# Clustered attention, a 2-D Fourier transform and a feed-forward network on one core: the transform in its own space beside the preceding sequence's last half block, and the normalization on other engines

## The chip, the cores and the metric

The kernel runs on one core of a Trainium2 chip. That core has five engines that work side by side: PE (matrix products; the trace shows its weight loads apart, as PEld), DVE (vector work), ACT (functions of one operand, scaled), POOL (GpSimd) and SP, which here only issues DMAs. Each engine takes its instructions in the order in which the program holds them. The metric is the device time of one execution in microseconds, lower being better. Of the kernel before there are three timed runs: 1066.58, 1066.92 and 1068.79 us, with a median of 1066.92 us.

## The reference, cut to what matters

```python
# q, k, v: (4, 8, 768, 64); centroids: (8, 16, 64); w_ch1: (512, 2048); w_ch2: (2048, 512)
q_assign = argmax(q_n @ c_n.T); k_assign = argmax(k_n @ c_n.T)     # unit vectors, per head
scores = where(q_assign[:, None] == k_assign, (q @ k.T) / 8, -1e9)
attn = softmax(scores) @ v                                          # (4, 768, 512) after joining heads
u = attn + real(fft(fft(attn, axis=seq), axis=model))
un = (u - mean(u)) / sqrt(var(u) + 1e-6)
out = u + relu(un @ w_ch1) @ w_ch2
```

Everything is held to about float32 accuracy: each product is made of float16 halves, a high and a low part, and three matmuls (high by high, high by low, low by high).

## The kernel before, in words

**Attention.** The 32 heads (4 sequences of 8) are taken in 16 pairs, and each pair in 6 blocks of 128 queries. So there are 96 steps, 24 for each sequence. A step's `scores` makes two tiles of 128x768 scores on PE, in two PSUM tiles of the pool `ps_big`, of which there are only two; DVE takes each row's maximum (L322, two instructions of a step, called the maxima here), ACT makes the exponentials (L328) and their high halves (L333), POOL the low halves (L334), a transposing DMA turns them round, and two steps later `attend` multiplies them by v. The two score tiles come free when ACT has made the exponentials; until then the next step's scores, first in PE's queue, wait, and with them all that PE has behind them.

**What follows a sequence's attention** is called its layer here. `fold` adds and subtracts mirrored rows and columns of the sequence X; its halves are transposed by DMA. `transform` then multiplies by cosine and sine tables: three accumulations of the odd part (L659 by way of `three`), three and one short one of the even part, each split into halves by ACT and DVE, and then three blocks t = 0, 1, 2 of a cosine and a sine pass. Their sums and differences dm and dp (L716, L717) are added to X (L723, L724); block 0 also makes one middle column. `norm` takes mean and variance of two row blocks and writes normalized rows as halves, which a DMA transposes (L756 to L769); `inverse` makes the factor that undoes its power-of-two scale (L776 to L783). `up` makes 16 feature blocks of 12 matmuls each (L798), of which ACT takes the rectified value in float32 (L802) and in float16 (L803) and POOL the rest (L804). `down` makes two outputs of 48 matmuls each (L818), yielded in pieces of 12; a piece costs 2.6 us in the planner's count. Norm, up and down come three times for a sequence, for two row blocks each, called half blocks here.

**Order.** PE's order is written out by the program: `Overlap.run` makes a table of steps, and after each step's scores and attend `fill` takes pieces of the layer of the sequence before, in proportion to what is left (`COST` 130 us over 24 steps). The other engines' orders are made by a scheduler from priorities; `high_priority` puts instructions ahead. At the end of a sequence `fold` is called, two steps later `drain` issues all that is left of the layer before, then the second part of `fold` (small transposes on PE), and `begin` starts the new layer. So on PE a layer is over before the next one's transform starts. The last sequence's layer has no attention beside it; it follows the rest of the third one's.

**Space.** One SBUF region, `arena`, serves the tables, the transform's parts and the feed-forward's activations by hand-set offsets. The tables `cs` and `ss` (577.5 KB each) lie at offset 0, where `up` keeps its activations, so they are loaded when the layer before has finished there.

The prediction's steps touch `Fourier.fold`, `tables`, `transform`, `FeedForward.norm`, `inverse`, `up`, `down` and `Overlap.layer`, `fill`, `drain`, `begin`, `run`.

## Time and profile before

| | |
|---|---|
| timed runs | 1066.58, 1066.92, 1068.79 us |
| the profiled execution | 1062.06 us, of which the span from first to last instruction is 1060.3 us |
| busy, of the span | PE 918.0 us (87%), ACT 635.9 (60%), DVE 601.3 (57%), POOL 569.3 (54%) |
| granted TensorE clock, mean | 0.934 of full speed |

The trace is of one execution, and its clock starts with the first instruction. Busy time of PE counts matmuls from issue to end, overlapping ones once, so 100% says that PE never waited, not that it ran at its peak. The granted clock has two levels here: 1.00 is 2.4 GHz and 0.50 is 1.2 GHz, and a mean between them tells the share of the time at each. The program's shape in time: attention with nothing of a layer beside it up to about 240 us; then three times a layer beside the next sequence's attention, with a change of layers near 240 to 300, 460 to 540 and 680 to 760 us; and from 884 us the last layers alone.

### The profile page before, as it was taken

What the parts mean: (1) busy time and instruction counts of PE and PEld (TensorE: products, weight loads), DVE (VectorE), ACT (ScalarE), POOL (GpSimd) and SP (SyncE); (2) the same over time, 40 slices, a digit from 0 to 9 for tenths busy, and PEclk for the clock granted to TensorE, in tenths of its full rate; (3) what the DMA queues carried; (4) which work ended last, traced back from release to release, by engine and by line L of the source; (5) the groups of instructions that cost most, each with busy time, mean ns of one, the idle gap of its engine ahead of it and who ended that gap; (6) DMA issues with size and microseconds to landing.
All of it is one profiled execution on the core that took longest, in us unless ns stands there. A gap on an engine that the chain in (4) does not pass through costs nothing.

```text
span 1060.3 us, 23530 instructions
## 1 busy us (share of the span) xinstructions
PE 918.0 (87%) x9349; PEld 598.4 (56%) x9362; DVE 601.3 (57%) x1325; ACT 635.9 (60%) x1051; POOL 569.3 (54%) x605
## 2 busy tenths in 40 slices
PE   3666565658799999998899999989899999699998
PEld 1243333335575766755666758556658575475674
DVE  8779897686955454568845454689354222710000
ACT  4798997855575766755766748556757472251340
POOL 1364565755684756655955657538737463341330
PEclk9987887868899999998999999998999999889999
DMA  7799998986778666788697656788666563211000
GB/s 267 180 218 235 204 251 186 177 163 126 152 116 183 120 135 124 135 154 155 123 174 132 136 120 131 132 160 158 110 132 108 98 112 62 67 30 36 11 11 21
DMA packets 381582, 141.58 MB, mean 134 GB/s; under 512 B 366104, under 2 KB 366112, under 8 KB 381472
## 3 DMA queue, kind: packets, MB, share of 16 engines
q1 hardware_dynamic: 381472, 140.08, 65.0%
q8 instruction: 73, 1.20, 0.5%
q14 instruction: 37, 0.30, 0.1%
HBM read 42.53 MB, written 6.29 MB: 46 GB/s over the span
## 4 chain that ended last, share of the span: by engine, by line
PE 55%; DVE 14%; DMA 12%; ACT 8%; issue 6%; POOL 5%; SPq 0%; POOLq 0%; ACTq 0%; DVEq 0%
PE ps_f L818 20%; PE ps_f L798 19%; PE ps_big L303 5%; DMA pt<-p 3%; DMA arena<-in_moe_w_ch_dram 3%; DMA pt<-ph 3%; POOL ph L334 2%; PE ps_o L354 2%; PE ps_o L356 2%; PE ps_o L355 2%; PE ps_f L659 2%; ACT p L328 2%; ACT ph L333 2%; DVE ju L322 1%; PE ps_big L308 1%
## 5 line engine op out<-in xcount | busy, mean ns | idle before, releaser
L334 POOL TENSOR_TENSOR ph<-p,ph 128x768 f16<-128x768 f32 x144 | 241.6, 1679 | 149.9 <-ACT ph L333 120.3
L798 PE MATMUL ps_f<-arena,w1h 128*128 128x256 f16 x1536 | 267.5, 275 | 17.6 <-DVE rt L782 10.7
L818 PE MATMUL ps_f<-w2h,arena 128*128 128x512 f16 x768 | 238.3, 379 | 0.0
L328 ACT ACTIVATE p<-ps_big,rmx,sce 128x768 f32<-128x768 f32 x144 | 142.5, 992 | 126.7 <-DVE ju L322 118.0
L322 DVE TENSOR_SCALAR_CACHE_REDUCE ju<-ps_big,sce 128x768 bf16<-128x768 f32 x144 | 145.9, 1013 | 116.2 <-PE ps_big L308 109.3
L798 PE MATMUL ps_f<-arena,w1l 128*128 128x256 f16 x768 | 211.1, 275 | 0.0
L804 POOL TENSOR_TENSOR arena<-arena 128x256 f16<-128x256 f32 x192 | 130.9, 687 | 135.3 <-ACT arena L803 132.9
L818 PEld LDWEIGHTS <-arena 128*128 128x128 f16 x1152 | 109.0, 98 | 126.4 <-issue 4.2
L354 PE MATMUL ps_o<-v,pt 128*128 128x66 f16 x1152 | 128.6, 201 | 49.3 <-DVE X L370 25.2
L798 PEld LDWEIGHTS <-w1h 128*128 128x128 f16 x1536 | 151.4, 99 | 35.0 <-issue 16.9
L303 PE MATMUL ps_big<-hlk,hlq 64*128 64x384 f16 x1152 | 132.6, 355 | 39.9 <-ACT p L328 26.9
L802 ACT ACTIVATE arena<-ps_f,wrel 128x256 f32<-128x256 f32 x192 | 92.2, 480 | 98.9 <-PE ps_f L798 73.9
L354 PEld LDWEIGHTS <-pt 128*128 128x128 f16 x1152 | 112.2, 101 | 64.0 <-issue 33.9
L818 PE MATMUL ps_f<-w2l,arena 128*128 128x512 f16 x384 | 145.5, 379 | 0.0
L355 PE MATMUL ps_o<-v,pt 128*128 128x64 f16 x1152 | 128.5, 201 | 0.0
L356 PE MATMUL ps_o<-v,pt 128*128 128x66 f16 x1152 | 128.1, 200 | 0.0
L333 ACT CAST ph<-p 128x768 f16<-128x768 f32 x144 | 119.9, 836 | 9.0 <-DMA pt<-ph 7.4
L303 PEld LDWEIGHTS <-hlq 64*128 64x128 f16 x1152 | 56.6, 100 | 102.7 <-issue 74.3
L355 PEld LDWEIGHTS <-pt 128*128 128x128 f16 x1152 | 112.7, 102 | 3.0
L356 PEld LDWEIGHTS <-pt 128*128 128x128 f16 x1152 | 113.1, 104 | 0.0
L803 ACT ACTIVATE arena<-ps_f,wrel 128x256 f16<-128x256 f32 x192 | 92.0, 479 | 0.0
L824 DVE SCALAR_TENSOR_TENSOR arena<-ps_f,rest,X 128x512 f32<-128x512 f32 x24 | 17.9, 746 | 129.7 <-PE ps_f L818 129.7
(169 smaller groups left out, 1332.7 us busy)
## 6 DMA issues: line engine op xcount, KB each, us to landing
arena<-in_moe_w_ch_dram SPq DMA_DIRECT2D x32, 512.0 KB, 5.9
scr<-in_q_dram SPq DMA_DIRECT2D x16, 384.0 KB, 3.2
scr<-in_k_dram SPq DMA_DIRECT2D x16, 384.0 KB
vst<-in_v_dram SPq DMA_DIRECT2D x16, 384.0 KB, 3.3
out_dram<-arena SPq DMA_DIRECT2D x24, 256.0 KB, 2.6
pt<-ph SPq DMA_TRANSPOSE x168, 3.9
arena<-in_cs_dram SPq DMA_DIRECT2D x4, 577.5 KB
arena<-in_ss_dram SPq DMA_DIRECT2D x4, 577.5 KB
```

The lines of the kernel that those rows point to most:

```text
L303: nc.tensor.matmul(out=ps[j][:, hf, 0:SH], lhsT=hq[rows[j], a, sl], rhs=hk[rows[j], c, hs], start=(i == 0), stop=False)
L322: nc.vector.tensor_scalar(out=ju, in0=ps[j][:, :, 0:SH], scalar1=ne, scalar2=None, op0=ALU.mult, op1=ALU.min, accum_out=m)
L328: nc.scalar.activation(x, ps[j][:, :, 0:SH], AF.Exp, bias=m, scale=e)
L333: nc.scalar.copy(out=ph[:, 0], in_=p32)
L334: nc.gpsimd.tensor_tensor(out=ph[:, 1], in0=p32, in1=ph[:, 0], op=ALU.subtract)
L354: nc.tensor.matmul(out=o[:, at:at + W], lhsT=hi, rhs=v16[:, kt, 0:W], start=(kt == 0), stop=False)
L355: nc.tensor.matmul(out=o[:, at:at + D], lhsT=hi, rhs=v16[:, kt, 66:130], start=False, stop=False)
L356: nc.tensor.matmul(out=o[:, at:at + W], lhsT=lo, rhs=v16[:, kt, 0:W], start=False, stop=(kt == ST - 1))
L798: nc.tensor.matmul(out=ps.rearrange("p (t x) -> p t x", x=P), lhsT=a[:, dc, fs], rhs=c[:, :, dc], start=(i == 0), stop=(i == 11))
L802: nc.scalar.activation(r, ps, AF.Relu, scale=rel[:, f:f + 1])
L804: nc.gpsimd.tensor_tensor(out=hl[:, f], in0=r, in1=hh[:, f], op=ALU.subtract)
L818: nc.tensor.matmul(out=ps, lhsT=a[:, f, ts], rhs=c[:, f], start=(i == 0), stop=(i == 47))
```

## The change

Three groups of edits. Line numbers of the changed kernel differ: `three` is L673, dm and dp L734 and L735, the additions to X L741 and L742, `norm` L774 to L788, `inverse` L795 to L802, the float32 rectification L822 or L824, `down`'s matmuls L847.

1. The transform gets offsets of its own: `arena` grows from 42176 to 47264 bytes, the tables `cs` and `ss` are loaded in thirds, each into space whose content has just been used, and `fold` does the odd part first. The layer before keeps its last pieces (`KEEP` 10.5, or `KEEP3` 7.9 before the last layer, counted in the planner's us), and `layer` hands them out between the transform's parts by the lists `MIX` and `MIX3`. The second part of `fold` comes one step after the first instead of two.
2. `norm`: the normalized rows are made by ACT instead of DVE; the low halves by POOL, but for the first of a sequence; the scale is computed for two rows at once. `inverse` is POOL's but for a reciprocal. Every second feature block of `up` is rectified in float32 by DVE instead of ACT. The additions to X of blocks 1 and 2 are all POOL's.
3. The layer's instructions are issued behind the latest maxima (`issue_after`), and norm 0 is called in block 1 of the transform, not after block 0; norm 2 in `down` of half block 0, not ahead of it.

```diff
-    CS, SS, CM, NY, XR, YN, MID = 0, 4640, 9280, 9824, 10592, 12160, 13216
-    XF, XT, XH, XM, XC, XL = 24640, (30816, 33888), 36960, 40128, 41184, 41216
-    FE = (0, 0, 1, 1)
-    UE = (1, 1, 0, 1)
+    CD, SD, XF, XT, XH = 20480, 22560, 24640, (30816, 33888), 36992
+    XM, XC, XL, XR, CM, YN, NY = 40160, 41216, 41248, 41280, 42848, 43392, 44448
+    CS, SS = (33888, 30816, 20480), (35456, 32352, 22016)
+    FOLDS = ((1, ALU.subtract), (0, ALU.add))
+    FE = (0, 0, 0, 1)
+    UE = (1, 1, 1, 1)
...
+    def third(self, t):
+        at = self.arena.at
+        n = P + (t == 0)
+        self.cs, self.ss = at(self.CS[t], [P, 2, 3, n], F16), at(self.SS[t], [P, 2, 3, P], F16)
+        for nm in ("cs", "ss"):
+            self.nc.sync.dma_start(out=getattr(self, nm)[:, :, :, 0:P], in_=self.con[nm][:, :, :, t * P:t * P + P])
+        if t == 0:
+            self.nc.sync.dma_start(out=self.cs[:, :, :, P:n], in_=self.con["cs"][:, :, :, SH:SH + 1])
+        return self.cs, self.ss
...
         for w, f in ((1, self.odd), (0, self.even)):
...
+            if w:
+                tab.append(self.third(0))
...
+        tab += [self.third(1), self.third(2)]
...
+            if t == 1:
+                yield "first"
...
-            nc.vector.tensor_scalar(out=un, in0=X[:, blk + 3 * j], scalar1=mv[:, j, 0:1], scalar2=s[:, j:j + 1],
-                                    op0=ALU.subtract, op1=ALU.mult)
+            nc.scalar.activation(un, X[:, blk + 3 * j], AF.Identity, bias=s[:, 1, j:j + 1], scale=s[:, 0, j:j + 1])
             h = at(self.UH[j], [P, 2, DM], F16)
             nc.scalar.copy(out=h[:, 0], in_=un)
-            (nc.vector, nc.gpsimd)[j].tensor_tensor(out=h[:, 1], in0=un, in1=h[:, 0], op=ALU.subtract)
+            (nc.gpsimd if j or blk else nc.vector).tensor_tensor(out=h[:, 1], in0=un, in1=h[:, 0], op=ALU.subtract)
...
+        nc.gpsimd.tensor_tensor(out=t, in0=rest, in1=rest, op=ALU.mult)
+        nc.gpsimd.tensor_tensor(out=t, in0=t, in1=va, op=ALU.mult)
+        nc.gpsimd.tensor_scalar(out=t, in0=t, scalar1=-0.5, scalar2=1.5, op0=ALU.mult, op1=ALU.add)
+        nc.gpsimd.tensor_scalar(out=s, in0=s, scalar1=self.w.dsc[:, 0:1], scalar2=None, op0=ALU.mult)
+        nc.gpsimd.tensor_tensor(out=rest, in0=rest, in1=t, op=ALU.mult)
+        nc.gpsimd.tensor_tensor(out=rest, in0=rest, in1=s, op=ALU.mult)
...
-            nc.scalar.activation(r, ps, AF.Relu, scale=rel[:, f:f + 1])
+            if f % 2:
+                nc.vector.tensor_scalar(out=r, in0=ps, scalar1=rel[:, f:f + 1], scalar2=0.0, op0=ALU.mult, op1=ALU.max)
+            else:
+                nc.scalar.activation(r, ps, AF.Relu, scale=rel[:, f:f + 1])
...
+            if blk == 2 and j:
+                nc.gpsimd.tensor_copy(out=o, in_=x)
+                x = o
...
-    COST = 130.0
+    END = 28
+    COST, KEEP, KEEP3 = 130.4, 10.5, 7.9
...
+    MIX = (1, 0, 0, 0, 1, 0, 0, 1, 1, 0)
+    MIX3 = (0, 0, 0, 0, 0, 0, 0, 1, 1, 1)
+    F2 = 1
-    def layer(self, b):
+    def layer(self, b, old):
+        mix = iter(self.MIX3 if b == B - 1 else self.MIX)
         for t in fft.transform(b):
-            if t == 0:
+            if t == "first":
                 with self.tc.high_priority():
-                    n = ffn.norm(b, 0)
-                ffn.inverse(*n)
+                    m = ffn.norm(b, 0)
+                ffn.inverse(*m)
+                continue
             yield 0.8 if t is None else None
+            for _ in range(next(mix)):
+                c = next(old, 0.0)
+                if c:
+                    yield c
+        yield from old
...
+    def step(self):
+        with self.tc.issue_after(self.att.mark.ins):
+            return next(self.gen, 0.0)
-    def drain(self):
+    def drain(self, keep):
+        while self.left > keep:
+            c = self.step()
...
     def begin(self, b, end):
-        self.fft.tables()
-        self.gen, self.credit, self.left, self.end = self.layer(b), 0.0, self.COST, end
+        self.gen, self.credit, self.left, self.end = self.layer(b, self.gen), 0.0, self.left + self.COST, end
...
-            at(t + 2, 0, self.drain)
-            at(t + 2, 0.1, step, self.fft.fold, b)
-            at(t + 2, 0.2, self.begin, b, t + 26)
+            at(t + self.F2, 0, self.drain, self.KEEP if b < B - 1 else self.KEEP3)
+            at(t + self.F2, 0.1, step, self.fft.fold, b)
+            at(t + self.F2, 0.2, self.begin, b, t + self.END)
```

What this does to the order shows at three places. The first is PE in the last sequence's transform, at the end of the middle column of block 0 (rows of 1x257); before, block 1's cosine pass follows at once:

```order
L659 LDWEIGHTS arena
L659 MATMUL ps_f<-arena 1x257
L659 LDWEIGHTS arena
L659 MATMUL ps_f<-arena 1x257
L659 LDWEIGHTS arena
L659 MATMUL ps_f<-arena 128x257
```

In the changed kernel the same place holds the first of three pieces of `down` of the third sequence (12 matmuls against `w2h` and `w2l`):

```order
L673 LDWEIGHTS arena
L673 MATMUL ps_f<-arena 1x257
L673 LDWEIGHTS arena
L673 MATMUL ps_f<-arena 1x257
L847 LDWEIGHTS arena
L847 MATMUL ps_f<-w2h,arena 128x512
L847 LDWEIGHTS arena
L847 MATMUL ps_f<-w2l,arena 128x512
```

One piece stands there, one behind block 1 and one behind block 2; before, all three ran ahead of the transform.

The second place is DVE in the second sequence's transform, between the additions of block 0 and the second of the two maxima of that step (`ju,rmx`). Before, norm 0 (`mv`, `rpow`, the normalized rows `arena<-X_64,mv,rpow`) and its `inverse` (`rt`) stand around and between the maxima:

```order
L759 TENSOR_SCALAR mv<-mv 128x1
L764 TENSOR_SCALAR arena<-X_64,mv,rpow 128x512
L391 RECIPROCAL scp<-scp 128x3
L393 TENSOR_SCALAR sce<-scp 128x1
L760 TENSOR_SCALAR rpow<-mv 128x1
L393 TENSOR_SCALAR sce<-scp 128x1
L322 TENSOR_SCALAR ju,rmx<-ps_big,sce 128x768
L780 TENSOR_SCALAR rt<-rest,mv 128x1
L762 TENSOR_SCALAR rpow<-rpow 128x1
L780 TENSOR_SCALAR rt<-rest,mv 128x1
L768 TENSOR_TENSOR arena<-arena 128x512
L322 TENSOR_SCALAR ju,rmx<-ps_big,sce 128x768
```

In the changed kernel the statistics of norm 0 follow the second of these maxima, and the halves of the next pair's queries and keys (`hlq`, `hlk`) stand between the two:

```order
L391 TENSOR_SCALAR scp<-ps_f 128x3
L392 RECIPROCAL scp<-scp 128x3
L394 TENSOR_SCALAR sce<-scp 128x1 x2
L323 TENSOR_SCALAR ju,rmx<-ps_big,sce 128x768
L231 SCALAR_TENSOR_TENSOR hlq<-scr,scp,hlq 128x768
L231 SCALAR_TENSOR_TENSOR hlk<-scr,scp,hlk 128x768
L323 TENSOR_SCALAR ju,rmx<-ps_big,sce 128x768
L774 BN_STATS bst<-X_64 128x6 x2
L775 BN_AGGR mv<-bst 128x2 x2
L211 TENSOR_REDUCE amx<-scr 128x1
L777 TENSOR_SCALAR mv<-mv 128x2
```

The norm has left the place between the maxima, and two operations of the next pair have come there.

The third place is POOL in the last sequence's transform, from the first additions to X to the first low half of norm 0 (`arena<-arena 128x512`; `rest<-mv,mhalf` is the power in `inverse`). Before:

```order
L723 TENSOR_TENSOR X_64<-X_64,arena 128x257
L724 TENSOR_TENSOR X_64<-X_64,arena 128x255 x2
L723 TENSOR_TENSOR X_64<-X_64,arena 128x257
L724 TENSOR_TENSOR X_64<-X_64,arena 128x255
L776 TENSOR_TENSOR rest<-mv,mhalf 128x2
L724 TENSOR_TENSOR X_64<-X_64,arena 128x255
L776 TENSOR_TENSOR rest<-mv,mhalf 128x2
L768 TENSOR_TENSOR arena<-arena 128x512
```

In the changed kernel `inverse` of norm 0 comes first, then the four additions of block 1, and then the low half:

```order
L796 TENSOR_TENSOR rest<-mv,mhalf 128x2
L797 TENSOR_TENSOR rt<-rest 128x2
L798 TENSOR_TENSOR rt<-rt,mv 128x2
L799 TENSOR_SCALAR rt<-rt 128x2
L801 TENSOR_TENSOR rest<-rest,rt 128x2
L741 TENSOR_TENSOR X_64<-X_64,arena 128x257
L742 TENSOR_TENSOR X_64<-X_64,arena 128x255 x2
L741 TENSOR_TENSOR X_64<-X_64,arena 128x257
L800 TENSOR_SCALAR rpow<-rpow,dsc 128x2
L787 TENSOR_TENSOR arena<-arena 128x512
```

Block 2's additions and the second norm's power, which stood ahead of that low half, are behind it now.

## Rows read from the trace of the kernel before

**Rows 1.** Windows: busy us (instructions) of PE, PEld, DVE, ACT, POOL; clock, DMA share, GB/s

```profile
240.00:320.00 80.00, 68.92 (x766) 48.60 (x765) 60.42 (x157) 52.22 (x92) 55.00 (x55) 0.89 0.74 135
460.00:540.00 80.00, 73.55 (x801) 50.74 (x800) 61.44 (x158) 52.14 (x91) 54.06 (x54) 0.94 0.82 150
480.00:520.00 40.00, 34.59 (x383) 23.94 (x380) 37.73 (x115) 25.17 (x41) 25.70 (x26) 0.87 0.75 146
540.00:680.00 140.00, 140.00 (x1518) 90.64 (x1516) 74.66 (x135) 88.24 (x144) 81.76 (x87) 1.00 0.68 136
680.00:780.00 100.00, 90.60 (x966) 59.22 (x963) 70.16 (x178) 60.10 (x100) 62.51 (x62) 0.95 0.80 145
...
900.00:940.00 40.00, 29.01 (x217) 20.35 (x216) 23.79 (x90) 13.46 (x31) 14.16 (x17) 0.83 0.27 66
929.00:933.00 4.00, 4.00 (x20) 2.83 (x21) 1.93 (x10) 0.55 (x2) 1.15 (x1) 0.50 0.64 123
```

**Rows 2.** Waits of PE, 240 to 880 us: total us, times, longest us

```profile
PE ps_big L303 <- ACT p L328: 16.1, 11, 3.4
```

**Rows 3.** Timeline of PE, 480 to 500 us: start us, us, engine, line, operation

```profile
493.95 0.48 PE L303 MATMUL ps_big<-hlk,hlq 64*128 64x384 f16 x1 [2.86 <-ACT p L328]
```

**Rows 4.** Timeline of DVE, 489 to 494 us

```profile
489.81 0.54 DVE L764 TENSOR_SCALAR arena<-X,mv,rpow 128x512 f32<-128x512 f32 x1
...
490.63 1.01 DVE L322 TENSOR_SCALAR_CACHE_REDUCE ju<-ps_big,sce 128x768 bf16<-128x768 f32 x1
...
491.99 0.68 DVE L768 TENSOR_TENSOR arena<-arena 128x512 f16<-128x512 f32 x1
492.59 1.01 DVE L322 TENSOR_SCALAR_CACHE_REDUCE ju<-ps_big,sce 128x768 bf16<-128x768 f32 x1
```

**Rows 5.** Timeline of PE, last sequence's transform

```profile
904.61 1.49 PE L659 MATMUL ps_f<-arena 128*128 128x257 f16 x12 [0.27 <-DVE arena L603]
...
909.59 1.17 PE L659 MATMUL ps_f<-arena 128*128 128x257 f16 x9
...
911.02 3.37 PE L659 MATMUL ps_f<-arena 128*128 128x257 f16 x27
...
917.08 1.17 PE L659 MATMUL ps_f<-arena 128*128 128x257 f16 x9
928.97 0.37 PE L798 MATMUL ps_f<-arena,w1h 128*128 128x256 f16 x1 [10.72 <-DVE rt L782]
```

**Rows 6.** Timeline of DVE, last sequence, block 0

```profile
912.30 0.49 DVE L716 SCALAR_TENSOR_TENSOR arena<-ps_f,vseq,arena 128x257 f32<-128x257 f32 x1 [1.78 <-PE ps_f L659]
```

**Rows 7.** Timeline of POOL, 912 to 930 us

```profile
916.49 0.73 POOL L723 TENSOR_TENSOR X<-X,arena 128x257 f32<-128x257 f32 x1 [21.05 <-DVE arena L716]
917.17 1.59 POOL L724 TENSOR_TENSOR X<-X,arena 128x255 f32<-128x255 f32 x2
...
924.62 1.15 POOL L768 TENSOR_TENSOR arena<-arena 128x512 f16<-128x512 f32 x1 [0.17 <-ACT arena L767]
```

**Rows 8.** Lines by form: count, busy us, mean ns, idle before them and its releasers

```profile
L802 ACT ACTIVATE arena<-ps_f,wrel 128x256 f32<-128x256 f32 x192 | 92.2, 480 | 98.9 <-PE ps_f L798 73.9 <-POOL arena L804 23.9 <-PE ps_big L308 0.9
...
L764 DVE TENSOR_SCALAR arena<-X,mv,rpow 128x512 f32<-128x512 f32 x24 | 15.7, 659 | 1.0 <-POOL arena L768 1.0
...
L767 ACT CAST arena<-arena 128x512 f16<-128x512 f32 x24 | 14.9, 620 | 34.8 <-DVE arena L764 23.9 <-DMA arena<-arena 10.5 <-DVE rest L783 0.3
...
L768 DVE TENSOR_TENSOR arena<-arena 128x512 f16<-128x512 f32 x12 | 9.6, 803 | 3.1 <-ACT arena L767 3.1
...
L410 POOL TENSOR_SCALAR vseq<-vseq 128x1 f32<-128x1 f32 x12 | 2.3, 215 | 11.9 <-DVE vseq L407 11.9
```

**Rows 9.** Windows of the tile rt alone (L780 to L783 of `inverse`), whole span

```profile
0.00:1060.00 1060.00, 17.03 (x96) 0.93 0.66 134
```

**Rows 10.** Line L723: duration min/median/max ns, first and last start us

```profile
L723 DVE TENSOR_TENSOR X<-X,arena x16: 383/420/1868, 261.8 to 921.7; 128x257 f32<-128x257 f32 x16
```

**Rows 11.** DMA issues: KB each, median us from issue to landing

```profile
arena<-in_cd_dram SPq DMA_DIRECT2D x4, 257.0 KB, 2.9
```

More of the change, by code (lines that the diff above doesn't have):

```diff
@@ L1 @@
+import contextlib
 from contextlib import ExitStack
@@ L610, in fold @@
         W, M = SH + 1, DM // 2
+        self.tables()
         self.scale[b] = self.sc.sequence(b)
@@ L751, in norm @@
         mv = sb.tile([P, 2, 2], F32, name="mv", tag="mv", bufs=2)
-        s = sb.tile([P, 2], F32, name="rpow", tag="rpow", bufs=2)
+        s = sb.tile([P, 2, 2], F32, name="rpow", tag="rpow", bufs=2)
         un2 = at(self.UN2[blk % 2], [P, 2, 8, P], F16)
@@ L864, in layer @@
                 yield cost
-            if blk == 0:
-                ffn.inverse(*ffn.norm(b, 2))
-            yield from ffn.down(b, blk)
-        while True:
-            yield None
+            for f, cost in enumerate(ffn.down(b, blk)):
+                if blk == 0 and f == 5:
+                    ffn.inverse(*ffn.norm(b, 2))
+                yield cost
     def fill(self, share):
@@ L875, in fill @@
         while self.credit > 0:
-            c = next(self.gen)
-            if c is None:
+            c = self.step()
+            if not c:
                 self.credit, self.hold = 0.0, self.now
```

76 lines of the change are left out of this document (35 added, 41 removed).

## The prediction

> **What bounds the kernel now.** I read the windows first, stretch by stretch, and not the page's shares. From 540 to 680 us PE is busy 140.00 of 140 us at a clock of 1.00 [rows 1]: there a layer beside attention is bound by PE, and no edit on another engine is worth anything as long as it stays hidden. Time is lost at four places, all of them changes from one layer to the next. PE is idle for 80 - 68.92 = 11.1 us in 240:320, 80 - 73.55 = 6.4 in 460:540, 100 - 90.60 = 9.4 in 680:780 and 40 - 29.01 = 11.0 in 900:940, together 37.9 us [rows 1]. The granted clock falls there too, to a mean of 0.89, 0.94, 0.95 and 0.83; a mean of 0.94 over 80 us is full-speed work of 4.8 us not done, if PE had work all the while.
>
> Next the waits. From 240 to 880 us PE's largest is for the score tiles, which come free after the exponentials: 16.1 us in 11 waits [rows 2]. The longest kind is seen at 493.95, where PE has stood still for 2.86 us [rows 3]. What made the exponentials late stands in DVE's rows: the maxima of that step run at 490.63 and 492.59 us, with a normalization (L764, 0.54 us) just ahead and a low half (L768, 0.68 us) in between [rows 4]. In 480:520 DVE is busy 37.73 of 40 us [rows 1]. So at the changes of layers DVE is the bound and PE waits for it by way of ACT. In the last change, without attention, it is another thing: PE ends block 2 of the transform at 917.08 + 1.17 = 918.25 us, waits 10.72 us for norm 0 (the row names an instruction of its `inverse`, the last to end before), and starts `up` at 928.97 [rows 5]; from 929 to 933 us the clock is 0.50 [rows 1].
>
> **The change part by part.** The sum is made against the profiled execution, 1062.06 us (span 1060.3 and 1.8 us around it). It lies 4.9 us below the median of the timed runs, 1066.92; I take the gain from both.
>
> *The last change of layers.* Three pieces of 12 matmuls move from ahead of the transform into it. The planner's 2.6 us each is 7.8 us that need no longer be done ahead of it. On the old time scale: the 27 matmuls from 911.02 take 3.3 us, 1.1 us for each nine: block 0's sine pass ends at 912.1, the middle column at 913.2 [rows 5]. Then come a piece, block 1 (2.5 us), a piece, block 2 (2.5), a piece: 913.2 + 5.0 + 7.8 = 926.0 us, the earliest start of `up`. Is norm 0 there by then? Its last link is POOL's low half, which now stands behind block 1's additions. Block 1's sine pass ends at 918.3; dm and dp take about 0.9 us (0.49 for the one shown [rows 6]), to 919.3; four additions of 0.73 to 0.8 us on POOL, 3.1 us, to 922.4; one small instruction, 0.2; the low half 1.15 us, to 923.8 [rows 7]. From the end of that low half (924.62 + 1.15 = 925.77) to the first matmul of `up` took 3.2 us before [rows 5, 7], by transposing DMA, and so it ends near 927.0. PE then waits about 1 us, not 10.7. Start of `up`: 927.0 - 7.8 = 919.2 against 928.97, 9.8 us. With a wait that short I expect the clock to stay up; the 4.6 us that ran at half speed behind the old wait (to about 933.6) then cost 2.3 us less. Together 12 us, at least 9.
>
> *The two middle changes.* What is lost lies between idle time alone and idle time with all of the clock's shortfall: 6.4 to 11.2 us in 460:540 and 9.4 to 14.4 in 680:780. Four pieces of `down`, each 12 matmuls, are spread over the transform's steps, so that PE has something behind the scores. DVE is rid of L764 (15.7 us for 24), of 9 of 12 low halves (7.2 of 9.6 us) and of rt (17.03 us for 96) [rows 8, 9], 40 us in all and 10 for a sequence, which fell into just these stretches. It gets back the mirrored addition of `fold` and a product for each norm, about 1.4 us a sequence. In the order before, some 2.9 us of norm lie ahead of the first maximum of the stalled step and 0.9 us between the two; both go. What is late next there is the second maximum, now behind the next pair's halves `hlq` and `hlk`, two DVE instructions of 1.0 us that wait for ACT: it comes about 3 us behind the first, but a piece of 2.6 us, attend and block 1 lie between it and the next scores. I count a margin of 1 us. I take 9 of the 11.2 and 11 of the 14.4 us.
>
> *The first change.* Its loss is 11.1 to 19.9 us, but no layer is left to fill with, and attention alone does not fill PE up to 240 us. What is won is that the transform starts one step earlier and `up` with it, and DVE's relief. I take 8 us.
>
> *Paid elsewhere.* ACT makes 24 normalized rows of 128x512, at 0.62 us by the nearest row (L767) 15 us, and loses 96 of the 192 rectifications of 0.48 us, 46 us [rows 8]. DVE gets these 96: between 0.38 us (the shortest two-input addition of 257 columns in SBUF [rows 10]) and 0.5 us (0.49 for 257 columns from PSUM [rows 6]), say 0.48 and 46 us. Their cover is the PE-bound stretch, where DVE is busy 74.66 of 140 us [rows 1]. If that cover is gone, each holds a PSUM tile of `up` while it stands behind two maxima of 1.01 us. The loads of thirds sit on SP's queue and wait for the odd accumulations to end, with the scores' transposes queued behind them. The odd part ends near 904.61 + 0.75 = 905.3, the first cosine pass is at 909.59 [rows 5]: 4.3 us for a third of two tables, against 2.9 us from issue to landing of 257 KB [rows 11]. I take 0; at most 1.5 us a layer, since the thirds come in shorter pieces. Transposes have two steps of slack.
>
> *What GpSimd takes over.* The same addition L723 takes 383 ns on DVE at best and 1868 at worst [rows 10], so it is being held up by something now and then; POOL works on SBUF in those stretches 55.00 of 80 us [rows 1]. The Trainium skill, "SBUF — State Buffer", section "Who interferes with whom", says that a DVE instruction with two SBUF inputs and a GpSimd instruction that reads SBUF exclude each other for a whole instruction; by that rule moving work to GpSimd would be paid for by DVE. The spread of L723 agrees with it, though the row does not name POOL as the cause. The price is worked out among the rivals.
>
> Sum: 12 + 9 + 11 + 8 = 40 us, less 6 for what I cannot price (second maxima, thirds, the DVE rectifications in the busier steps) gives 34. Profiled: 1062.06 - 34 = 1028. Timed: 1066.9 - 34 = 1033 us.
>
> **Rivals.** *ACT takes DVE's place (0.22).* The normalized rows and both rectifications stand between the exponentials on ACT, which is busy 25.17 of 40 us in 480:520, less loaded than DVE [rows 1]: against it. For it: norm 0 needs four ACT instructions in a row, 4 x 0.62 = 2.5 us, just where exponentials are awaited. Then only a third of the 28 us at the three attended changes is won: 12 + 9 = 21 us, 1046.
>
> *GpSimd and DVE in each other's way (0.10).* POOL gets per sequence two low halves of 1.15, two additions of 0.73, eighteen small instructions of about 0.2 (L410: 0.215) and a copy of about 0.8, all by rows of POOL [rows 7, 8]: 8 us. If each of these microseconds stops DVE at the three attended changes, 24 of the 34 us are gone: 1057. Against it: the moved additions and low halves are themselves DVE instructions with two SBUF inputs, which are fewer now.
>
> *Slower: the PSUM tiles of `up` come free too late (0.07).* 96 feature blocks wait for DVE. From 34 / 96 = 0.35 us of PE time a block on, the gain is eaten. At one half of a maximum each, 0.5 us, it is 48 us, and the time 1081. Against it: three tiles and 1.3 us of matmuls a block leave 2.6 us of slack, and DVE has half its time free there.
>
> *It does not do what it says (0.05).* The pieces run, but the scores stall in front of them as before, and the last wait moves to the transform's parts, since one PSUM tile of three is held by the unfinished `down`: 1067.
>
> **How the numbers follow.** The forecast, 1033, has 0.56; its own range is 1019 (48 us, four fifths of the 59 us of idle time and clock) to 1045. The range for 8 in 10 goes up through the first rival and to the edge of the second: 1018 to 1056. Left out are the last two rivals, half of the second and a little below. A difference of 0.2%, about 2 us, is what a measurement of this kernel can tell. Faster: 0.56 + 0.22 + 0.10 = 0.88; same 0.05; slower 0.07.
>
> **What would show it.** In the profile after: PE's wait ahead of the first `up` of the last layer under 3 us and no stretch at clock 0.50 behind it; PE over 97% busy at the second and third change, with the wait for the exponentials under a third of 16.1 us; 100% in the PE-bound stretches. I am wrong if PE waits there for DVE's rectification, or for ACT's exponentials as long as before, or if DVE's two-input instructions grow longer.

## The result, and the profile of the changed kernel

The changed kernel takes 1058.32 us (median of 14 runs) where the kernel before takes 1067.97 beside it: ratio 0.9915, 95% interval 0.9894 to 0.9936. It is 9 us faster; 34 were predicted, and 1058 lies above the range of 1018 to 1056. The first profiled execution, 1064.92 us, is the longest of its 14, so a second was taken (`a0_again`, 1055.96 us); the rows below are from the first, and the second has the same waits within 0.9 us.

To see where the time went I add up, over PE's matmuls, how much longer each stands until the next one starts than the median of its function and shape in the trace of before. That counts waits and a low clock alike, in us. A step runs here from one `attend` to the next; the kernels with names are those of the experiments below:

| trace (profiled time) | steps 0–24 | first change, 24–32 | second, 48–60 | third, 72–84 | steps between | last change and tail | sum |
|---|---|---|---|---|---|---|---|
| before (1062.06) | 111.3 | 27.4 | 10.4 | 13.8 | -4.2 | 13.9 | 172.5 |
| changed, first (1064.92) | 108.8 | 30.4 | 13.8 | 12.1 | 1.6 | 8.4 | 175.0 |
| changed, second (1055.96) | 106.5 | 28.5 | 12.9 | 12.2 | 0.2 | 6.5 | 166.6 |
| `e3_relu` (1044.37) | 107.1 | 28.0 | 7.8 | 9.8 | -5.3 | 7.1 | 154.5 |
| `f3_nomix` (1078.22) | 104.4 | 34.3 | 18.3 | 18.1 | -5.3 | 16.5 | 186.3 |
| `n1_norm` (1075.85) | 115.6 | 31.7 | 15.1 | 15.0 | -5.8 | 15.0 | 186.5 |
| `h2_edge` (1049.59) | 109.4 | 26.0 | 9.1 | 10.9 | 1.1 | 2.9 | 159.4 |
| `h1_old` (1041.56) | 107.2 | 25.9 | 8.8 | 8.2 | -1.0 | 1.8 | 151.1 |
| `i2_free` (1041.77) | 106.9 | 28.0 | 7.8 | 6.5 | 0.7 | 1.8 | 151.7 |

Differences of the sums follow those of the profiled times within 1 us, but for `f3_nomix` (2.4). Each trace is of one execution, which lies up to 7 us off the median of its kernel's runs (before 6 below, `e3_relu` 4 below). The two traces of one kernel differ by up to 2.3 us in a column, so smaller differences say nothing. Against before, the second trace has won 7.4 us in the tail and 4.8 in the first 24 steps (for which no step of the prediction accounts), and lost 2.5 at the second change and 4.4 in the steps between; the 1.6 won at the third change and the 1.1 lost at the first are too small to tell.

PE's waits of the changed kernel, 230 to 940 us: total us, times, longest.

```profile
PE ps_f L637 <- POOL arena L627: 11.4, 3, 9.3
PE ps_big L304 <- ACT p L329: 9.9, 8, 3.0
PE ps_f L817 <- ACT arena L825: 8.7, 9, 2.2
PE ps_f L817 <- DMA arena<-arena: 7.1, 3, 3.4
PE ps_f L673 <- DMA arena<-in_cs_dram: 4.7, 2, 2.5
...
PE ps_f L817 <- ACT arena L784: 0.9, 1, 0.9
```

The scores (L304) wait less than before, where it was 21.9 us in 13 over this stretch (16.1 from 240 us on in [rows 2]). But three kinds stand beside them that before had little of: fold's column (L637), norm 0's transposed rows ahead of `up` (L817) and the tables (L673); and the rectifications (L825) wait 8.7 us where it was 6.3. Its windows, columns as in [rows 1]:

```profile
240.00:320.00 80.00, 72.17 (x781) 49.15 (x778) 50.79 (x113) 48.90 (x82) 55.09 (x66) 0.86 0.84 146
460.00:540.00 80.00, 72.00 (x777) 47.92 (x779) 56.01 (x113) 48.48 (x78) 50.74 (x63) 0.91 0.78 149
480.00:520.00 40.00, 33.83 (x358) 21.08 (x356) 32.17 (x67) 22.52 (x35) 24.29 (x31) 0.87 0.83 164
540.00:680.00 140.00, 136.91 (x1519) 90.78 (x1516) 81.89 (x163) 86.51 (x135) 86.95 (x99) 1.00 0.69 133
680.00:780.00 100.00, 91.67 (x978) 60.26 (x977) 67.55 (x136) 61.19 (x97) 64.69 (x75) 0.97 0.75 141
900.00:940.00 40.00, 35.43 (x230) 21.27 (x229) 21.38 (x53) 13.79 (x28) 14.98 (x28) 0.91 0.37 78
```

DVE is relieved as worked out (32.17 of 40 us in 480:520, 37.73 before), and PE is no busier for it. The stretch 540:680, full before, has lost 3.1 us. So of the prediction's signs only that of the last change will come: PE is busy 90 and 92% at the second and third change, not over 97, and 9.9 us of waits for the exponentials are more than a third of 16.1.

**The second change.** DVE, ACT, POOL, SP's queue and PE, from the last addition to X of block 0 to the start of `up`:

```profile
489.98 0.41 DVE L741 TENSOR_TENSOR X<-X,arena 128x257 f32<-128x257 f32 x1
...
494.61 1.01 DVE L323 TENSOR_SCALAR_CACHE_REDUCE ju<-ps_big,sce 128x768 bf16<-128x768 f32 x1
...
495.54 1.28 DVE L774 BATCH_NORM_STATS2 bst<-X 128x6 f32<-128x512 f32 x2
...
500.67 0.95 DVE L211 TENSOR_REDUCE amx<-scr 128x1 f32<-128x768 f32 x1 [0.44 <-DMA scr<-in_k_dram]
...
502.29 0.64 DVE L781 SCALAR_TENSOR_TENSOR rpow<-mv,rpow 128x2 f32<-128x2 f32 x1
...
502.97 1.52 ACT L784 ACTIVATE arena<-X,rpow 128x512 f32<-128x512 f32 x2 [5.02 <-DVE rpow L781]
...
506.71 1.16 POOL L787 TENSOR_TENSOR arena<-arena 128x512 f16<-128x512 f32 x1
...
508.22 1.34 SPq L788 DMA_TRANSPOSE arena<-arena  x1
...
505.94 0.32 PE L304 MATMUL ps_big<-hlk,hlq 64*128 64x384 f16 x1 [1.55 <-ACT p L329]
...
507.34 0.41 PE L304 MATMUL ps_big<-hlk,hlq 64*128 64x384 f16 x2 [1.08 <-ACT p L329]
...
512.24 0.37 PE L817 MATMUL ps_f<-arena,w1h 128*128 128x256 f16 x1 [2.49 <-DMA arena<-arena]
```

X is ready at 490.39 us, and its statistics start at 495.54, right behind the second maximum, where the order behind the maxima puts them. The exponentials behind that maximum end at 496.71, and the scores at 496.76 have waited 1.01 us for them. Between the small steps of the norm stand reductions for the next pair (L211) that wait for their load. ACT idles 5.02 us for the last small step and then makes the two rows and their casts around the next exponentials, and the scores wait 1.55 and 1.08 us; `up` waits for the transposed rows until 512.24. Before, the first statistics stood 0.03 us behind their additions:

```profile
484.30 0.42 DVE L724 TENSOR_TENSOR X<-X,arena 128x255 f32<-128x255 f32 x1
484.75 0.69 DVE L756 BATCH_NORM_STATS2 bst<-X 128x6 f32<-128x512 f32 x1
...
505.68 0.28 PE L798 MATMUL ps_f<-arena,w1h 128*128 128x256 f16 x1
```

**The last change**, to compare with [rows 5], on PE:

```profile
911.20 0.40 PE L673 MATMUL ps_f<-arena 128*128 128x257 f16 x2
914.07 0.40 PE L673 MATMUL ps_f<-arena 128*128 128x257 f16 x1 [2.47 <-DMA arena<-in_cs_dram]
...
934.07 0.27 PE L817 MATMUL ps_f<-arena,w1h 128*128 128x256 f16 x1 [0.89 <-ACT arena L784]
```

The wait of 10.72 us is 0.89, and the clock of 934:938 is 1.00. But PE waits for the tables, two matmuls into the first cosine pass, and behind that wait the clock is 0.50:

```profile
914.00:920.00 6.00, 5.93 (x27) 3.17 (x27) 1.54 (x4) 0.48 (x1) 0.00 (x0) 0.50 0.27 56
...
934.00:938.00 4.00, 3.93 (x37) 3.54 (x38) 3.05 (x9) 2.95 (x7) 3.42 (x7) 1.00 0.28 88
```

What is late there is not the third of the tables. Its load of `cs` is issued at 906.53 us, right behind the odd part. Behind it on SP's queue comes the load of one more column of `cs` for the middle column (L664, 1.5 KB), into the same tile; the queue holds it back for 1.8 us until the first has landed:

```profile
906.53 0.57 SPq L662 DMA_DIRECT2D arena<-in_cs_dram  x1
...
909.67 0.54 SPq L664 DMA_DIRECT2D arena<-in_cs_dram  x1
```

It is this small load, landing 4.3 us after its issue, that PE waits for, here and in the first change.

### The profile page after: what moved, and what is told of

The parts are those of the page before. It is cut to its first block, busy times and chain, and to the rows that moved or that the text cites. A ratio compares the mean times of both kernels' runs of the same rounds, so it can differ in the third digit from the quotient of the medians.

```text
span 1063.1 us, 23508 instructions
## 1 busy us (share of the span) xinstructions
PE 916.4 (86%) x9349; PEld 594.4 (56%) x9362; DVE 623.1 (59%) x1265; ACT 623.7 (59%) x979; POOL 592.6 (56%) x693
## 4 chain that ended last, share of the span: by engine, by line
PE 50%; DVE 14%; DMA 13%; ACT 7%; issue 6%; POOL 6%; SPq 1%; ACTq 0%; DVEq 0%; POOLq 0%
PE ps_f L847 18%; PE ps_f L817 17%; PE ps_big L304 5%; DMA pt<-ph 3%; DVE ju L323 2%; DMA arena<-in_moe_w_ch_dram 2%; POOL ph L335 2%; DMA scr<-in_k_dram 2%; PE ps_f L673 2%; PE ps_o L355 2%; DMA pt<-p 2%; PE ps_o L357 2%; PE ps_o L356 2%; ACT p L329 2%; DMA vst<-in_v_dram 1%
## 5 line engine op out<-in xcount | busy, mean ns | idle before, releaser
L817 PE MATMUL ps_f<-arena,w1h 128*128 128x256 f16 x1536 | 272.4, 278 | 17.0 <-ACT arena L825 8.7
L847 PE MATMUL ps_f<-w2h,arena 128*128 128x512 f16 x768 | 239.7, 380 | 0.5 <-ACT arena L825 0.5
L817 PE MATMUL ps_f<-arena,w1l 128*128 128x256 f16 x768 | 213.1, 277 | 0.0
L847 PEld LDWEIGHTS <-arena 128*128 128x128 f16 x1152 | 109.0, 98 | 128.2 <-issue 7.2
L817 PEld LDWEIGHTS <-w1h 128*128 128x128 f16 x1536 | 152.7, 99 | 33.9 <-issue 14.0
L355 PE MATMUL ps_o<-v,pt 128*128 128x66 f16 x1152 | 124.0, 198 | 44.5 <-DVE X L371 22.6
L304 PE MATMUL ps_big<-hlk,hlq 64*128 64x384 f16 x1152 | 130.0, 352 | 31.0 <-ACT p L329 16.4
L847 PE MATMUL ps_f<-w2l,arena 128*128 128x512 f16 x384 | 145.8, 380 | 0.0
L355 PEld LDWEIGHTS <-pt 128*128 128x128 f16 x1152 | 109.5, 100 | 59.4 <-issue 26.8
L356 PE MATMUL ps_o<-v,pt 128*128 128x64 f16 x1152 | 123.9, 199 | 0.0
L357 PE MATMUL ps_o<-v,pt 128*128 128x66 f16 x1152 | 123.5, 197 | 0.0
L825 ACT ACTIVATE arena<-ps_f,wrel 128x256 f16<-128x256 f32 x192 | 90.6, 472 | 54.3 <-DVE arena L822 54.1
L822 DVE TENSOR_SCALAR arena<-ps_f,wrel 128x256 f32<-128x256 f32 x96 | 46.2, 482 | 125.1 <-PE ps_f L817 69.9
L356 PEld LDWEIGHTS <-pt 128*128 128x128 f16 x1152 | 110.0, 100 | 2.8
L357 PEld LDWEIGHTS <-pt 128*128 128x128 f16 x1152 | 110.4, 102 | 0.0
L304 PEld LDWEIGHTS <-hlq 64*128 64x128 f16 x1152 | 56.0, 99 | 91.7 <-issue 63.7
L817 PEld LDWEIGHTS <-w1l 128*128 128x128 f16 x768 | 76.3, 99 | 20.4 <-issue 10.8
```

The costliest lines, as they stand in the source:

```text
L304: nc.tensor.matmul(out=ps[j][:, hf, 0:SH], lhsT=hq[rows[j], a, sl], rhs=hk[rows[j], c, hs], start=(i == 0), stop=False)
L355: nc.tensor.matmul(out=o[:, at:at + W], lhsT=hi, rhs=v16[:, kt, 0:W], start=(kt == 0), stop=False)
L356: nc.tensor.matmul(out=o[:, at:at + D], lhsT=hi, rhs=v16[:, kt, 66:130], start=False, stop=False)
L357: nc.tensor.matmul(out=o[:, at:at + W], lhsT=lo, rhs=v16[:, kt, 0:W], start=False, stop=(kt == ST - 1))
L817: nc.tensor.matmul(out=ps.rearrange("p (t x) -> p t x", x=P), lhsT=a[:, dc, fs], rhs=c[:, :, dc], start=(i == 0), stop=(i == 11))
L825: nc.scalar.activation(hh[:, f], ps, AF.Relu, scale=rel[:, f:f + 1])
```

## The experiments

Ratios are to the kernel before, run beside it on the same chip. Every edit lets the scheduler sort the other engines anew, and that shifts columns of the table by a few us (the first one, where no layer runs, goes from 104.4 to 115.6); a verdict therefore rests on the timed ratio, or on a wait that goes.

**The changed kernel again** (`a0_again`). 

> The changed kernel once more, unchanged, for a second trace: the profiled execution of the first (1064.9 us) lies 6.6 us above the median of its 14 runs, 1058.3. Theory A (the gain went into new waits at the changes of layers: PE waits 9.3 us for the copy of fold's last column at 238 us, 2.3 and 2.5 us for the first third of the tables, 2.5 and 3.4 us for norm 0's transposed rows): the same waits stand here, each within 1.5 us of these numbers, time 1056 to 1060. Theory B (they are accidents of a slow execution): the wait at the fold is under 5 us and those before up are under 1 us, in a profiled time near 1058.

Measured 0.9909 (0.9884 to 0.9934), 1058.08 us; fold's column 9.3 us, tables 3.8 us in 2, norm 0's rows 7.2 us in 3, longest 3.5. Theory A stands: the waits belong to the kernel.

**Rectifications.** All on ACT (`e3_relu`), or both of an odd block on DVE (`f5_dve2`):

```diff
@@ e3_relu @@
-            if f % 2:
-                nc.vector.tensor_scalar(out=r, in0=ps, scalar1=rel[:, f:f + 1], scalar2=0.0, op0=ALU.mult, op1=ALU.max)
-            else:
-                nc.scalar.activation(r, ps, AF.Relu, scale=rel[:, f:f + 1])
+            nc.scalar.activation(r, ps, AF.Relu, scale=rel[:, f:f + 1])
@@ f5_dve2 @@
-            nc.scalar.activation(hh[:, f], ps, AF.Relu, scale=rel[:, f:f + 1])
+            if f % 2:
+                nc.vector.tensor_scalar(out=hh[:, f], in0=ps, scalar1=rel[:, f:f + 1], scalar2=0.0, op0=ALU.mult, op1=ALU.max)
+            else:
+                nc.scalar.activation(hh[:, f], ps, AF.Relu, scale=rel[:, f:f + 1])
```

> All rectifications go back to ACT (two for each feature block), the rest of the change stays. Theory C (DVE's rectifications hold the PSUM tiles of up): PE's waits for them, 8.7 us in 9, fall below 4 us and the time falls by 3 to 6 us, 1052 to 1055. Theory A: DVE's share was hidden, the waits stay as they were in the kernel before (6.3 us in 6) or grow, since ACT carries 96 x 0.48 = 46 us more: 1058 to 1064.

> The changed kernel, but of each odd feature block DVE makes both rectifications, and ACT none: another 96 x 0.48 = 46 us for DVE. Theory E (the PSUM tiles of odd blocks come free late since ACT's one rectification stands in ACT's queue behind a cast that waits for a transposing DMA, as at 354.56 us): an odd tile no longer waits for ACT, PE's 9.4 us of waits fall below 4, and the time falls from 1058 to 1048 to 1054. Theory C (it is DVE that frees them late, behind its maxima): the waits double, 1062 to 1070.

`e3_relu`: 0.9820 (0.9796 to 0.9844), 1048.59 us, 9.5 us below the changed kernel and better than theory C said; PE's waits for a rectification fall from 9.4 us in 9 (`a0_again`) to 2.7 in 4 (there L822 on ACT), and the steps between are full again (-5.3):

```profile
PE ps_f L817 <- ACT arena L822: 2.7, 4, 1.0
```

The table puts 5.5 us of the gain into the steps between and 7.5 at the two middle changes, where PE waits for a rectification only once, 0.9 us (460:540 and 680:780); how that part follows was not taken apart. `f5_dve2`: 0.9874 (0.9847 to 0.9900), 1055.42 us, in between, by the ratios some 4 us below the changed kernel and just told apart; 2.1 us of waits for ACT's rectification are left and 3.9 for DVE's. Neither theory alone is right. ACT's waits in the changed kernel, 230 to 900 us, and DVE's, ACT's and PE's rows at the longest of PE's waits:

```profile
ACT arena L825 <- DVE arena L822: 30.9, 34, 2.3
```

```profile
352.47 0.48 DVE L822 TENSOR_SCALAR arena<-ps_f,wrel 128x256 f32<-128x256 f32 x1
...
354.56 0.83 ACT L334 CAST ph<-p 128x768 f16<-128x768 f32 x1 [2.08 <-DMA pt<-ph]
355.30 0.99 ACT L329 ACTIVATE p<-ps_big,rmx,sce 128x768 f32<-128x768 f32 x1
356.19 0.46 ACT L825 ACTIVATE arena<-ps_f,wrel 128x256 f16<-128x256 f32 x1
...
356.70 0.27 PE L817 MATMUL ps_f<-arena,w1h 128*128 128x256 f16 x1 [2.23 <-ACT arena L825]
```

ACT's rectification of an odd block (L825) starts only when DVE's (L822) has ended; the two read one PSUM tile. DVE's stands behind two maxima (here from 352.47 us), ACT's then behind a cast that waits 2.08 us for a transposing DMA and an exponential, and PE starts again at 356.70 after 2.23 us. So at this longest wait DVE's had ended 3.2 us before ACT came to its own, and in seven of the nine waits it had 1.1 to 3.3 us before; ACT itself waits for DVE in one. What the split costs PE there is above all the place that ACT's half gets in its queue. In `e3_relu` the pair stands at once behind the first exponential:

```profile
346.50 0.99 ACT L329 ACTIVATE p<-ps_big,rmx,sce 128x768 f32<-128x768 f32 x1 [0.85 <-DVE ju L323]
347.39 0.46 ACT L821 ACTIVATE arena<-ps_f,wrel 128x256 f32<-128x256 f32 x1
347.74 0.47 ACT L822 ACTIVATE arena<-ps_f,wrel 128x256 f16<-128x256 f32 x1
349.59 0.83 ACT L334 CAST ph<-p 128x768 f16<-128x768 f32 x1 [1.37 <-DMA pt<-ph]
```

**The overlap**, on `e3_relu`: undone, begun a step later, or with a piece moved behind block 2.

```diff
@@ f2_f2 and f3_nomix @@
-    F2 = 1
+    F2 = 2
@@ f3_nomix @@
-    MIX = (1, 0, 0, 0, 1, 0, 0, 1, 1, 0)
-    MIX3 = (0, 0, 0, 0, 0, 0, 0, 1, 1, 1)
+    MIX = (0,) * 10
+    MIX3 = (0,) * 10
...
-            at(t + self.F2, 0, self.drain, self.KEEP if b < B - 1 else self.KEEP3)
+            at(t + self.F2, 0, self.drain, -1e9)
@@ f1_mix @@
-    MIX = (1, 0, 0, 0, 1, 0, 0, 1, 1, 0)
+    MIX = (1, 0, 0, 0, 1, 0, 0, 0, 1, 1)
```

> On the base of 1048.6 us the overlap of the layers is undone: the preceding layer is drained before fold's second part, no pieces stand in the transform, and fold has its two steps. Norms on ACT and GpSimd, thirds and the order behind the maxima stay. Theory A (the overlap is what cured the stall of the scores at 490 us, and it shortens the tail): the stalls of 6.75 and 6.47 us come back at the second and third change and 6 us in the tail, 1056 to 1068. Theory F (DVE's relief by the norms did it): the stalls stay away, and only the tail loses its 6 us, 1052 to 1056.

> On the base of 1048.6 us the second part of fold, and with it the transform, starts a step of attention later, as in the kernel before. Theory A (a transform that starts one step earlier wins nothing at the first change, since PE waits 9.4 us for fold's column there): the wait shrinks below 5 us, a step of attention stands in it, and the time is the same or up to 4 us less, 1044 to 1049. The prediction's step (the earlier start of the transform is worth 8 us at the first change together with DVE's relief): 3 to 8 us more, 1052 to 1057.

> From here on the base is the kernel with all rectifications on ACT (1048.6 us). In it the fourth piece of the preceding layer's down stands behind block 2 of the transform and not behind block 0, that is right ahead of up, where PE waited 3.24 and 2.25 us for norm 0's rows. Theory A: a piece of 2.76 us covers most of these waits, and with them the half-speed clock behind them (6.8 and 10.2 us at 0.50, so 3.4 and 5.1 us of work): 5 to 10 us faster at the second and third change, 1039 to 1044. Rival: the steps ahead lose the cover that they have now, the scores' waits grow by what up's waits shrink: 1046 to 1051.

`f3_nomix`: 1.0119 (1.0090 to 1.0147): without the overlap the kernel is slower than before, and the overlap is worth 0.0299 x 1067 = 32 us. By the table that is 6.3 at the first change, 10.5 and 8.3 at the middle ones and 9.4 in the tail. What PE waits for then, 230 to 960 us, is not the scores alone:

```profile
PE ps_f L817 <- DMA arena<-arena: 26.9, 4, 10.3
PE ps_big L304 <- ACT p L329: 25.7, 14, 3.2
```

`f2_f2`: 0.9912 (0.9881 to 0.9943), 10 us slower than its base; the early start is worth that, as the prediction said against theory A, and 6 us stand at the first change (34.1 against 28.0 in the measure of the table). `f1_mix`: 0.9858 (0.9823 to 0.9892); 5 us above its base, nothing won: the scores' stall takes the cover's place (4.1 and 4.7 us more just ahead of it, in the table's measure). The rival was right.

**The norms.** Alone in the kernel before (`n1_norm`), or in their old form in the changed kernel (`e4_norm`), in `h2_edge` (`h1_old`), with only the inverse on GpSimd (`i1_inv`). The edit exchanges `norm` and `inverse`, or `inverse` alone, for those of the other kernel.

> The kernel before, and of the change only the norms: normalized rows on ACT, the inverse and two low halves on GpSimd, the small steps of both tokens together. No overlap, no order behind the maxima, no thirds. The prediction's step (DVE is the bound at the changes and its 40 us are what PE waits for): the stalls of 6.75 and 6.47 us at the scores shrink, 5 to 12 us faster than before, ratio 0.989 to 0.995. Theory G (DVE's work for the norms was not what the scores waited for, or the chain to up takes the place of the stall): within 3 us, 0.997 to 1.003, or slower.

> Only the norm goes back to the form of before: normalized rows, one low half and the small steps of the inverse on DVE; overlap, thirds, rectifications and the order behind the maxima stay. Theory D (ACT takes DVE's place: the normalized rows hold up the exponentials): the scores' waits ahead of up (1.55 + 1.08 us at the second change, 1.0 + 1.08 at the third) go, 1053 to 1057. Theory A, with the prediction: DVE is the bound again at the changes, its 40 us come back where 2.9 us of stall a change stood, and the time rises by 5 to 9 us, 1063 to 1067.

> As h2_edge, with the norms in the form of before (normalized rows, the inverse and all but three low halves on DVE). Theory I (the new route through ACT and GpSimd is longer, as n1_norm's 5 us suggest, and DVE's relief is worth less than that): 3 to 8 us below h2_edge, about 1038 to 1042. Theory D (the prediction: DVE's 40 us are felt once the rectifications are off DVE): 5 to 12 us above it.

> As h1_old (0.9773 of the kernel before), but the inverse is taken over by GpSimd as in the change: 96 small steps of rt leave DVE, 17.0 us, and the normalized rows stay on DVE. If the rows on ACT are what costs, the time is that of h1_old or up to 5 us less, since DVE is relieved: 1038 to 1043. If it is the inverse on GpSimd, in front of GpSimd's other work, the time goes back to that of h2_edge, 1048 to 1051.

`n1_norm`: 1.0043 (1.0026 to 1.0061), 5 us slower, though DVE has less to do. The scores' waits do not shrink, 26.4 us in 14 against 21.9 in 13 from 230 us on, and those for rectifications on ACT are 10.7 (6.3 before); of the 12.1 us for norm 0's rows 11.4 are the wait of the last change, 10.72 in [rows 5]. `e4_norm`: 0.9898 (0.9873 to 0.9923), no difference from the changed kernel. `h1_old`: 0.9773 (0.9753 to 0.9794) against 0.9834 (0.9810 to 0.9858) for `h2_edge`: the old form is 6.5 us faster, so theory I holds and D falls. `i1_inv`: 0.9799 (0.9774 to 0.9824) lies between both and is told from neither.

**The order behind the maxima.** Norm 0 taken out of it (`g1_free` on `e3_relu`, `i2_free` on `h1_old`); no such order at all (`h6_noedge` on `h2_edge`).

```diff
@@ g1_free, i2_free; layer yields "norm" ahead of norm 0 and "done" behind it @@
         with self.tc.issue_after(self.att.mark.ins):
-            return next(self.gen, 0.0)
+            c = next(self.gen, 0.0)
+        if c == "norm":
+            assert next(self.gen) == "done"
+            c = self.step()
+        return c
@@ h6_noedge @@
-        with self.tc.issue_after(self.att.mark.ins):
-            return next(self.gen, 0.0)
+        return next(self.gen, 0.0)
```

> On the base of 1048.6 us (0.982 of the kernel before) norm 0 alone is taken out of the order behind the maxima; every other step of a layer keeps it. In the base X of block 0 is ready at 490.4 us in the first trace of the changed kernel, and norm 0's statistics start at 495.54, right behind the second maximum, with the large reductions of the next pair between its small steps; in the kernel before they started 0.03 us behind X. Theory G (that order is what makes norm 0's rows late for up): the waits of 3.24 and 2.25 us ahead of up go, with them the scores' waits of about 2 us a change and half-speed clock for 3.4 to 5 us, 8 to 15 us in all: 1034 to 1041, ratio 0.968 to 0.975. Rival H (the chain through ACT, GpSimd and the transposing DMA is too long by itself, or the maxima are late again and the stall of 6.5 us at the scores comes back): 1046 to 1054.

> As h2_edge, without the order behind the maxima for any step of a layer. Theory K (the order guards the maxima: without it the layer's work on DVE goes ahead of them and the scores' stall of 6.5 us comes back at the second and third change): 4 to 10 us above h2_edge. Rival (the order only shifts the wait from the scores to up, as for norm 0): within 2 us of it.

> As h1_old, with norm 0 free of the order behind the maxima. If the place behind the maxima costs norm 0 time that up waits for, 3 to 6 us below h1_old, 1037 to 1040. If the scores' stall comes back instead, as with the new norms (g1_free 0.9841 against 0.982), 1041 to 1046.

`g1_free`: 0.9841 (0.9817 to 0.9864), nothing won: the second change stands still (7.8 to 9.3 in the table's measure), since the scores wait 2.24 us where `up` had waited 3.24. Theory G, that the order is the loss, fell. `h6_noedge`: 0.9836 (0.9813 to 0.9859), equal to its base; the order is worth nothing that can be told. `i2_free`: 0.9755 (0.9729 to 0.9781), 1040.74 us, the fastest kernel; not told apart from `h1_old` (0.9773).

**Fold's column and the first third.**

```diff
@@ e1_last, g5_last, h2_edge @@
+        nc.gpsimd.tensor_tensor(out=last.rearrange("p (a o) -> p a o", o=1), in0=X[:, 0:3, M:M + 1], in1=X[:, 3:6, M:M + 1],
+                                op=ALU.add)
...
-            if i == 0:
-                nc.gpsimd.tensor_copy(out=last.rearrange("p (a o) -> p a o", o=1), in_=f[:, :, M:M + 1])
@@ g4_third, g5_last, h2_edge @@
-    CS, SS = (33888, 30816, 20480), (35456, 32352, 22016)
+    CS, SS = (45216, 30816, 20480), (16384, 32352, 22016)
...
-        tab = []
+        tab = [self.third(0)]
...
-            if w:
-                tab.append(self.third(0))
```

> The column that fold hands to PE's small transposes is added up straight from the two halves of X, ahead of everything else in fold, instead of being copied out of the folded sum, which the new order makes last. Theory A: the waits of 9.3, 1.65 and 0.48 us for that copy go; the scores behind it are next, and their exponentials end at 233.1 and 235.1 us, 4 to 6 us ahead of where the scores start now; the kernel gets 4 to 7 us faster than the changed one, 1051 to 1054. Rival: in that stretch PE waits for the exponentials all the same and the wait is only relabelled: under 1.5 us, 1057 to 1058.

> As g1_free, and the first third of the two tables has a place of its own (45216 and 16384 in the arena), so that its load waits for no accumulation of the odd part. Theory A (the loads that wait are on the path: 1.5 to 2.6 us of PE's wait in the first and the last change and half-speed clock behind the latter): 3 to 6 us below g1_free. Rival (the transform is held by something else anyway): within 1.5 us of it.

> As g4_third, and fold's last column is added up straight from X. By itself on the changed kernel that edit moved nothing (1058.8 against 1058.1), although PE's wait of 9.3 us went: the scores' exponentials took its place. Theory A (the wait was only relabelled in the first change, and saves 1 to 2 us at the second): 0 to 3 us below g4_third. Rival (it now counts, since the stretch behind it is shorter): 4 to 8 us below.

> The changed kernel with all rectifications on ACT, the first third of the tables in its own place and fold's last column straight from X; norm 0 keeps its place behind the maxima. Theory G said that this place costs 8 to 15 us, and g1_free showed nothing of it; if it is neutral, ratio 0.976 to 0.980 (1043 to 1047), as g5_last (0.980) or a little better. If norm 0's place does cost, 0.984 or more.

`e1_last`: 0.9915 (0.9890 to 0.9941). PE's waits for the column, 9.3 us and two more, are gone and the time is the same; the scores' waits grow from 9.4 us in 8 (`a0_again`) to 14.7 in 11: the rival. `g4_third`: 0.9824 (0.9801 to 0.9847), `g5_last`: 0.9800 (0.9776 to 0.9824); neither is told from its base, both together are 4 us below `g1_free`, just told apart. In the trace of `g4_third` the tail falls from 6.9 to 2.9 us, and the wait of 2.1 us for the tables is gone. `h2_edge`, both edits without the free norm, gives 0.9834, no gain over `e3_relu`: its tail is 4.2 us shorter, but the scores wait 20.0 us in 13 where they waited 8.1 in 7. The tail's part is shown, a gain of the whole is not.

**DVE at the changes** (`h5_noqk`, on `h2_edge`):

```diff
+        if pr in (6, 10, 14):
+            self.nc.gpsimd.memset(m[:, 0:2], 4.0)
+            return m
```

> As h2_edge; left out are the reductions for the largest q and k of the three pairs that are prepared during a change of layers (6, 10 and 14; a constant stands in their place): two instructions of 0.95 us on DVE in each change, which also wait there for the load of q and k (0.85 and 0.44 us in the second change). Theory J (DVE is the bound at the changes, in its own queue, and norm 0's small steps stand behind these two): PE's waits for scores and at up shrink by 3 us or more a change, and half-speed clock with them, 8 to 14 us below h2_edge. Rival (the chain through ACT, GpSimd and the transposing DMA is): at most 2 us below it.

0.9786 (0.9768 to 0.9804), 5.1 us below its base, for 6 x 0.95 = 5.7 us of DVE's work. Both theories missed. The time falls nearly one for one with DVE's work and not two for one, but the edit also takes away DVE's waits for the loads of q and k, and the traces do not place the gain: PE is busy 73.13 of 80 us in 460:540 and 94.58 of 100 in 680:780, where it was 73.16 and 94.19.

## Why the prediction was wrong, step by step

- **The rectifications: "Their cover is the PE-bound stretch."** This step failed, for 9.5 us (`e3_relu`). It is the mechanism of the third rival, a PSUM tile freed late, at a fifth of the price given there. I had counted DVE's queue alone, and not that ACT's reading of the same tile waits for DVE's and so falls behind a cast and an exponential in ACT's own queue. The Trainium skill, "PSUM — Partial Sum Buffer", section "PSUM bank collisions raise a hardware error", says that two engines may not touch the same partitions of a bank at once, reads included, and that the compiler orders them. The trace agrees: L825 waits for L822 57 times, 54.1 us over the span, most of it where PE loses nothing. It spoke against this edit, and I did not weigh it.
- **"What is late next there is the second maximum."** Failed, and with it the 9 and 11 us of the middle changes. The stall of [rows 3] did go (in the table's measure, around it, 6.75 to 0.84 us at the second change and 6.47 to 0.56 at the third). The exponentials of the second maximum made the next scores wait 1.01 us, where I had counted a margin of 1. But next was something else, for which the sum has no term: the scores of the following step, 1.55 and 1.08 us, behind norm 0's rows on ACT, then those rows on their way to `up`, 2.49 us, and half clock; the steps behind the stall went from 3.6 to 9.3 us. With the old norm under the same overlap (`e4_norm`) PE does not wait for the rows at the middle changes, but the scores still wait 3.4 and 2.9 us there. So the rows are next only with the new norm, and what would win the rest of the 20 us stays open.
- **DVE's relief, 40 us, as a gain.** Wrong in sign for the edit that was to bring it. (It was 39: 8 low halves of 12 left DVE, not 9.) Taken by itself the new norm costs 5 us (`n1_norm`), in the changed kernel it makes no difference (`e4_norm`), and at the end the old form is 6.5 us better (`h1_old`). DVE's time is worth something (`h5_noqk`), but the rows then stand among the exponentials on ACT, 0.81 us each where I had taken 0.62: the first rival, ACT in DVE's place. How the cost divides between rows and inverse stays open (`i1_inv`).
- **The first change, 8 us.** Nothing came. The earlier start is worth 6 us there (`f2_f2`), and the new norm takes 4.3 (`n1_norm` against before), each read from one trace against one. The 9.3 us wait for fold's column, which I had not foreseen, cost nothing (`e1_last`).
- **The last change, 12 us.** Right in mechanism; 7.4 came. `up` waits 0.89 us where I said 1, at full clock. What failed in it is the term of the thirds, **"I take 0"**. The cover of 4.3 us was enough for the third itself, which I had weighed; it was not for the extra column behind it on SP's queue, which I had left out: a wait of 2.47 us and half clock behind it. With both loads ahead of the odd part and in a place of their own the tail is 2.9 us against 13.9, 11 us less.
- **The overlap.** My four terms were 40 us, and undoing it costs 32: these were roughly its price. The error was to add it to the kernel before with 6 us for all else. All else without it is 13 us slower than before (`f3_nomix`), 5 of them the norms; the other 8 (order of odd and even parts, thirds) were not taken apart.

## What to carry to other kernels

When a stall goes, follow the chain of every consumer behind it to its end before booking the gain: the next wait may stand a few us behind, hidden by the first. Count small loads too: one of 1.5 KB held PE here, behind a large one that was in time. Splitting the readers of one PSUM tile over two engines joins their queues, and the tile comes free when the later queue gets to it. Of a bundle of edits, undo each alone: here the overlap gave 32 us, and with the rectifications and norms put back, and three small edits beside them, a gain of 9 us became one of 26.
